# Attention values with the values held in the array: every second head by 64x64 quadrants

## The chip, the cores and the metric

The kernel runs on one core of a Trainium2 chip. The core has a matrix engine (TensorE, PE in the profile; its weight loads are listed as PEld), VectorE (DVE), ScalarE (ACT), GpSimd (POOL) and SyncE (SP), which here only issues DMA transfers. Each engine takes its own instructions in program order, and they wait for each other by semaphores. The metric is the device time of one execution in microseconds (us).

## The reference

A layernorm of `x` (2048 x 640) feeds two branches: attention with 32 heads of 192 over a cache of 2048 keys and values, and a gated MLP of width 1536. The result is `x + attention * silu(mlp)`.

```python
xn = layernorm(x)
q = (xn @ wq).reshape(B, Sq, H, Dh)              # H = 32, Dh = 192
scores = einsum("bhqd,bhkd->bhqk", q, k_cache) * Dh ** -0.5
o = einsum("bhqk,bhkd->bhqd", softmax(scores), v_cache)
s = o.reshape(B, Sq, H * Dh) @ wo
g = silu(silu_gated_mlp(xn, w1, w3, w2))
out = x + s * g
```

## The kernel before

Nearly all of the time goes to a loop over heads `h`, in each over four **blocks** `qb` of 512 queries, and in each block over eight **steps** `p`. A step handles 256 keys: key tiles `p` and `p + 8` of 128, kept as the index `t` of 0 and 1. `ROWS` are the two halves of the 128 partitions, 0 to 63 and 64 to 127. All matmuls of the loop use 64 rows of the array and 128 columns; two of them, one on each half of the rows, run side by side.

In a step, `scores` (L472) makes the transposed scores, keys on partitions and queries along the row: the 192 dimensions are three parts of 64, so three pairs of matmuls with 512 columns fill a PSUM tile `st2` of 128x1024. `weights` (L488) is one Exp on ScalarE, with a bound of the scores (`nb`) in place of the row maximum, into a bf16 tile `pT2`; the pool `pp` has four. `values` (L519) loads 64x128 pieces of `pT2` into the array as weights and streams the values `vt`: 192 columns and one column of ones (set in L142), so the 193rd column of each output row is the sum of its probabilities. That is sixteen matmuls of 193 columns a step, in eight pairs, into two PSUM tiles `ob0` and `ob1` (`acc["o"]`), where the two halves of the rows keep apart sums (index `r`). The values of a step are two **parts**, put in the list `parts`; `advance` (L545) first issues the scores and the Exp of a step and then takes parts off the list until three (four where `extra` is given) are left, so the values run one to two steps behind the scores.

At the end of a block `evict` (L493) has VectorE copy one half sum (L500), add the other (L501), take the reciprocal of the ones column (L506), and multiply (L507) into a bf16 stage `ostage`, which holds two heads (`HG`) of one block; after the second head SP stores it to `o_scr`.

In the second step of each block `extra` runs `project_chunk` (L340) for the same block of the next head: twenty matmuls of 512 columns (L361) into a tile `ps`, two casts on VectorE (L363, L364), and copies on GpSimd (L367, L371) that put halves of the queries on the other partitions. `ps` and `st2` come from one pool, `ps_st`, of two buffers. A step later VectorE takes the maxima of the queries (L375), and in the later steps those of the next head's keys (`next_keys`, L386), both for the bound. `load_head` (L150) loads keys (a DMA transpose on SP), values and weights of the head after the next at the start of a head. In odd heads `swiglu_chunk` (L454) works on a piece of the MLP that rides along in the projection. Instructions wrapped in `pin` keep their program order.

After the loop come the rest of the MLP (L704, L911, L927) and the output product with `wo` (L847, L891), which reads `o_scr` by DMA transposes.

Of the kernel before, what the change touches and what calls it, by code (L numbers as in the profile page):

```python
# [30 lines left out]
def _kernel_impl(ctx, tc, A_x, A_k_cache, A_v_cache, A_wq, A_wo, B_w1, B_w3, B_w2, out):  # L31
# [124 lines left out]
    with ExitStack() as actx:  # L156
        qp = actx.enter_context(tc.tile_pool(name="qp", bufs=2))
        pp = actx.enter_context(tc.tile_pool(name="pp", bufs=4))
# [150 lines left out]
        def start_head(h):  # L309
            L = loads.pop(h)  # L310
            heads[h] = dict(
                h=h, L=L,
# [27 lines left out]
        def project_chunk(h, qb, cast=nc.vector.tensor_copy, mid=()):  # L340
# [6 lines left out]
            if h == 0 and qb > 0:  # L347
                by_halves(halves, lambda t, c: wq[:, t, c, :], qs, nc.scalar.copy if qb == 1 else nc.vector.tensor_copy, steps((parts.pop(0),), *mid))
# [8 lines left out]
            else:  # L357
                for s in range(2 * DC):
                    for t in range(2):
                        xs = xnT if s % 2 == t else xnS  # L360
                        pin(nc.tensor.matmul(halves[t], lhsT=wq[ROWS[t], s, :], rhs=xs[ROWS[t], s // 2, qs],  # L361
                                             start=(s == 0), stop=(s == 2 * DC - 1)))
            pin(cast(out=qA[:, qs], in_=halves[0]))  # L363
            pin(cast(out=qF[:, qs], in_=halves[1]))  # L364
# [107 lines left out]
        def scores(hd, qb, p, fill=(0, 0, 0), st2=None):  # L472
# [8 lines left out]
            for s, step in enumerate(steps):  # L481
                keep_busy(fill[s])
                for t, (k, q) in enumerate(step):
                    pin(nc.tensor.matmul(st2[:, t * 512:(t + 1) * 512], lhsT=k, rhs=q[ROWS[t], qs],  # L484
                                         start=(s == 0), stop=(s == 2)))
            return st2

        def weights(st2, nb):  # L488
            pT2 = pp.tile([P, 1024], BF16, tag="pT2", name="pT2")
            pin(nc.scalar.activation(out=pT2[:], in_=st2[:], func=ACT.Exp, scale=SCALE, bias=nb[:]))  # L490
            return pT2

        def evict(hd, qb, b, ob):  # L493
            h, hg = hd["h"], hd["h"] % HG
            if b == 0 and hg == 0:
                acc[qb] = stp.tile([P, 4, HG * DH], BF16, tag=f"ostage{qb}", name="ostage")
            ostage = acc[qb]
# [5 lines left out]
            def rest():  # L503
# [3 lines left out]
                pin(nc.vector.tensor_tensor(out=ostage[:, b * 2:b * 2 + 2, hg * DH:(hg + 1) * DH], in0=osum[:, :, 0:DH],  # L507
                                            in1=rl.unsqueeze(2).to_broadcast([P, 2, DH]), op=ALU.mult))
                if b == 1 and hg == HG - 1:
                    g0 = h - hg  # L510
# [117 lines left out]
        def next_part():  # L628
            parts.pop(0)()
# [517 lines left out]
```

## Time and profile before

| what | time |
|---|---|
| device time, median of 3 runs (lowest to highest) | 1936.98 us (1936.93 to 1937.15) |
| span of the profiled execution, first to last instruction | 1935.5 us |
| end of the last scores matmul (end of the loop over heads) | about 1644 us |
| one block in the middle of the loop | 12.67 us |
| Exp of one step (128x1024) on ScalarE, mean | 1.113 us |

A row of a group of instructions reads: line, engine, operation, names written and read, shapes, count; then busy time in us and the mean duration in ns; then the idle time of the engine just before them and what ended it. A row of the chain of waits or of the timeline begins with the start in us from the span's start and the duration in us; `x6` is the number of instructions merged into it. `64*128` on a matmul is the part of the array in use, rows by columns. Matmuls are pipelined: one of 512 columns is listed with 0.38 us, though the next pair begins 0.216 us later.

### The profile page before, as it was taken

Reading aid. Unit: us, or ns where it says so; the run is one execution under the profiler, and the core shown is the slowest. Engines: PE = TensorE matmul, PEld = TensorE weight load, DVE = VectorE, ACT = ScalarE, POOL = GpSimd, SP = SyncE. Lnnn points to the kernel's source line nnn. Section 1 sums busy time; section 2 is a strip of 40 time slices with the busy share of each in tenths; the row PEclk is TensorE's granted clock in tenths of the full one; section 3 lists DMA queues with packets and bytes.
Section 4 is the critical chain, followed back from the end, with each engine's and each line's share of the span. In section 5 each row is a group of like instructions: output and inputs, shape, how many; then the busy total and the mean of one; then the engine's idle time right before and its main releaser. Section 6 shows DMA issues by size and latency. Waiting matters only on the chain.

```text
span 1935.5 us, 59521 instructions
## 1 busy us (share of the span) xinstructions
PE 1927.5 (100%) x26720; PEld 1266.1 (65%) x26743; DVE 1091.5 (56%) x2240; ACT 1213.5 (63%) x1173; POOL 457.9 (24%) x757
## 2 busy tenths in 40 slices
PE   9999999999999999999999999999999999999999
PEld 5666666666666666666666677666666666454446
DVE  8665656565656565666655666656665655521111
ACT  7777777777767677777777777777777777210000
POOL 3432222222222222233222222222222220000000
PEclk9999999999999999999999999999999999999999
DMA  7621313121212222242223222213131102946763
GB/s 172 133 71 41 80 41 79 42 71 38 59 41 65 52 55 62 57 95 68 63 50 71 50 71 49 71 41 79 42 79 38 43 10 90 262 93 144 166 151 77
DMA packets 340355, 148.31 MB, mean 77 GB/s; under 512 B 291632, under 2 KB 333584, under 8 KB 340096
## 3 DMA queue, kind: packets, MB, share of 16 engines
q1 hardware_dynamic: 327152, 114.84, 25.7%
q0 software_dynamic: 8256, 24.58, 4.8%
q10 hardware_dynamic: 4688, 5.05, 0.8%
q8 instruction: 210, 3.44, 0.8%
q14 instruction: 49, 0.40, 0.1%
HBM read 54.26 MB, written 31.98 MB: 45 GB/s over the span
## 4 chain that ended last, share of the span: by engine, by line
PE 99%; ACT 0%; issue 0%; DVE 0%; POOL 0%
PE obank L530 35%; PE st L484 34%; PE ps L361 14%; PE ps_s L891 8%; PE ps_s L847 3%; PE ps_f L911 2%; PE ps_gu L704 1%; PE ps_f L927 1%; PE ps L729 0%; PE ps L330 0%; PE fill L207 0%; PE pst L272 0%; PE ps_gu L330 0%; ACT xnT L273 0%; POOL qS L367 0%
## 5 line engine op out<-in xcount | busy, mean ns | idle before, releaser
L490 ACT ACTIVATE pT<-st,nb 128x1024 bf16<-128x1024 f32 x1016 | 1130.8, 1113 | 435.1 <-PE st L484 434.7
L530 PEld LDWEIGHTS <-pT 64*128 64x128 bf16 x16384 | 713.8, 94 | 242.0 <-ACT pT L490 1.5
L530 PE MATMUL obank<-vt,pT 64*128 64x193 bf16 x16384 | 852.3, 243 | 0.2 <-ACT pT L490 0.2
L500 DVE COPY osum<-obank 128x386 f32<-128x386 f32 x256 | 142.4, 556 | 551.4 <-PE obank L530 551.4
L484 PE MATMUL st<-qS,KM 64*128 64x512 bf16 x1023 | 385.2, 377 | 0.5 <-POOL qS L367 0.5
L484 PE MATMUL st<-qD,KT 64*128 64x512 bf16 x1023 | 385.2, 377 | 0.0
L484 PE MATMUL st<-qS,KT 64*128 64x512 bf16 x1023 | 385.1, 376 | 0.1
L484 PE MATMUL st<-qA,KT 64*128 64x512 bf16 x1023 | 385.2, 377 | 0.0
L484 PE MATMUL st<-qA,KM 64*128 64x512 bf16 x1023 | 385.2, 376 | 0.0
L484 PE MATMUL st<-qF,KT 64*128 64x512 bf16 x1023 | 385.1, 376 | 0.0
L367 POOL COPY qS<-qA 64x512 bf16<-64x512 bf16 x256 | 189.4, 740 | 513.8 <-DVE qA L363 482.3
L484 PEld LDWEIGHTS <-KT 64*128 64x128 bf16 x4096 | 202.2, 94 | 135.8 <-issue 0.6
L361 PE MATMUL ps<-xnT,wq 64*128 64x512 bf16 x1240 | 288.1, 376 | 0.0
L361 PE MATMUL ps<-xnS,wq 64*128 64x512 bf16 x1240 | 287.0, 377 | 0.0
L361 PEld LDWEIGHTS <-wq 64*128 64x128 bf16 x2480 | 120.6, 94 | 116.2
L507 DVE TENSOR_TENSOR ostage<-osum,rl_all 128x384 bf16<-128x384 f32 x256 | 153.4, 599 | 8.8
L891 PE MATMUL ps_s<-oT,wo_sb 128*128 128x512 bf16 x705 | 154.9, 379 | 0.8
L501 DVE TENSOR_TENSOR osum<-osum,obank 128x386 f32<-128x386 f32 x256 | 142.6, 557 | 8.9
L891 PEld LDWEIGHTS <-wo_sb 128*128 128x128 bf16 x720 | 70.4, 98 | 85.0 <-issue 0.2
L386 DVE TENSOR_REDUCE st<-KT 128x1 f32<-128x512 bf16 (+1 forms) x189 | 122.0, 685 | 1.2
L484 PEld LDWEIGHTS <-KM 64*128 64x128 bf16 x2048 | 101.0, 94 | 16.5 <-issue 0.5
L105 POOL DMA_DIRECT2D wq<-in_A_wq_dram x62 | 45.7, 737 | 272.8 <-PE ps L361 260.4
(136 smaller groups left out, 1174.6 us busy)
## 6 DMA issues: line engine op xcount, KB each, us to landing
o_scr<-ostage SPq DMA_DIRECT2D x64, 384.0 KB, 2.8
vt<-in_A_v_cache_dram SPq DMA_DIRECT2D x62, 384.0 KB, 4.9
wo_sb<-in_A_wo_dram POOLq DMA_DIRECT2D x1, 7680.0 KB, 32.6
wq<-in_A_wq_dram POOLq DMA_DIRECT2D x31, 160.0 KB, 3.3
hT_scr<-hblk SPq DMA_DIRECT2D x16, 256.0 KB, 3.0
xnS<-xnT POOLq DMA_DIRECT2D x8, 320.0 KB, 7.0
wq<-in_B_w_dram POOLq DMA_DIRECT2D x31, 80.0 KB, 2.6
wq<-in_A_wq_dram POOLq DMA_DIRECT2D x31, 80.0 KB, 2.9
```

The costliest lines, as they stand in the source:

```text
L105: keep(nc.gpsimd.dma_start(out=wq[ROWS[t], :, c0:c1], in_=w.rearrange("(s p) d -> p s d", p=DT)))
L361: pin(nc.tensor.matmul(halves[t], lhsT=wq[ROWS[t], s, :], rhs=xs[ROWS[t], s // 2, qs], start=(s == 0), stop=(s == 2 * DC - 1)))
L367: keep(nc.gpsimd.tensor_copy(out=qS[ROWS[t], qs], in_=qA[ROWS[1 - t], qs]))
L386: pin(nc.vector.tensor_reduce(out=heads[h]["st"][:, j, k:k + 1], in_=heads[h]["L"]["KT"][:, j, c0:c1], axis=AX.X, op=ALU.max, apply_absolu ...
L484: pin(nc.tensor.matmul(st2[:, t * 512:(t + 1) * 512], lhsT=k, rhs=q[ROWS[t], qs], start=(s == 0), stop=(s == 2)))
L490: pin(nc.scalar.activation(out=pT2[:], in_=st2[:], func=ACT.Exp, scale=SCALE, bias=nb[:]))
L500: pin(nc.vector.tensor_copy(out=osum[:], in_=ov[:, 0, :, 0:DH + 1]))
L501: pin(nc.vector.tensor_tensor(out=osum[:], in0=osum[:], in1=ov[:, 1, :, 0:DH + 1], op=ALU.add))
L507: pin(nc.vector.tensor_tensor(out=ostage[:, b * 2:b * 2 + 2, hg * DH:(hg + 1) * DH], in0=osum[:, :, 0:DH], in1=rl.unsqueeze(2).to_broadcas ...
L530: pin(nc.tensor.matmul(acc["o"][b][:, r, (j % 2) * 256:(j % 2) * 256 + DH + 1], lhsT=pT2[ROWS[r], t * 512 + j * P:t * 512 + (j + 1) * P], ...
L847: pin(nc.tensor.matmul(ps, lhsT=oT[:, k, :], rhs=wo_sb[:, k, c0:c1], start=(k == 0), stop=(k == OC - 1)))
L891: pin(nc.tensor.matmul(ps_of[d], lhsT=wo_sb[:, k, d * P:(d + 1) * P], rhs=part(k // KQ)[:, k % KQ, :], start=(k == 0), stop=(k == OC - 1)))
```

## The change

In the even heads from 2 to 30 (`in_quads`, fifteen of 32) the roles in the values product are exchanged: 64x64 pieces of the values `vt` are loaded into the array, and the probabilities `pT2` stream past with 512 columns. Four such matmuls make a group, one for each quadrant (rows `r`, columns `c`); a step has three groups, `high(0)`, `high(1)` for the first 128 value dimensions and `low` for the last 64 of both key tiles. The output is now transposed, value dimensions on partitions. Scores, projections and the last MLP piece in these heads are issued as 64x64 quadrants as well, so twice as many matmuls; at the border between two heads the first two steps and the projection keep the shape of the head before (`before["quads"]`).

The ones column is not used there. VectorE adds up `pT2` instead (`row_sums`): pairs of steps, then joins, then the two key tiles, in bf16; SP turns the 128x512 result with a DMA transpose, and VectorE reduces it and takes the reciprocal (`scale`). At the end of a block ScalarE copies one half sum of the high part (`evict_high`), VectorE copies one and adds two (`evict_low`), and SP turns the 128x1024 bf16 result with a DMA transpose into `ox`. GpSimd adds the two key tiles' low parts and multiplies by the reciprocals into `ostage`. The steps of this work that belong to no fixed place are held in a list, `chores`, from which `do_chores` takes up to `QUOTA[p]` after step `p`; `clock` counts steps, and `scale` is due six steps after `ends`.

`pT2` now holds two steps, with three buffers in place of four. The second cast of a projection goes to ScalarE while a quadrant head runs. `step` takes the place of `advance` from head 1 on: it empties the list of the block before ahead of a projection, and keeps five parts waiting in quadrant heads (three elsewhere). `stage` and `staged` make and store `ostage` when both heads of a pair have delivered. The pools of the new tiles (`aq`) are closed in the last head, and the pool `hTp` of the MLP opens there instead of after head 0.

The core of the diff:

```diff
+    def in_quads(h):
+        return 1 < h < H - 1 and h % 2 == 0
...
-        pp = actx.enter_context(tc.tile_pool(name="pp", bufs=4))
+        pp = actx.enter_context(tc.tile_pool(name="pp", bufs=3))
...
+        def by_steps(halves, w, qs, quads):
+            for s in range(2 * DC):
+                for c in ROWS if quads else (slice(0, P),):
+                    for t in range(2):
+                        xs = xnT if s % 2 == t else xnS
+                        pin(nc.tensor.matmul(halves[t][c, :], lhsT=w[ROWS[t], s, c], rhs=xs[ROWS[t], s // 2, qs],
+                                             start=(s == 0), stop=(s == 2 * DC - 1)))
...
-                for s in range(2 * DC):
-                    for t in range(2):
-                        xs = xnT if s % 2 == t else xnS
-                        pin(nc.tensor.matmul(halves[t], lhsT=wq[ROWS[t], s, :], rhs=xs[ROWS[t], s // 2, qs],
-                                             start=(s == 0), stop=(s == 2 * DC - 1)))
+                by_steps(halves, wq, qs, quads)
             pin(cast(out=qA[:, qs], in_=halves[0]))
-            pin(cast(out=qF[:, qs], in_=halves[1]))
+            pin((cast_low or cast)(out=qF[:, qs], in_=halves[1]))
...
-                for t, (k, q) in enumerate(step):
-                    pin(nc.tensor.matmul(st2[:, t * 512:(t + 1) * 512], lhsT=k, rhs=q[ROWS[t], qs],
-                                         start=(s == 0), stop=(s == 2)))
+                for c in ROWS if quads else (slice(0, P),):
+                    for t, (k, q) in enumerate(step):
+                        pin(nc.tensor.matmul(st2[c, t * 512:(t + 1) * 512], lhsT=k[:, c], rhs=q[ROWS[t], qs],
+                                             start=(s == 0), stop=(s == 2)))
             return st2
 
-        def weights(st2, nb):
-            pT2 = pp.tile([P, 1024], BF16, tag="pT2", name="pT2")
-            pin(nc.scalar.activation(out=pT2[:], in_=st2[:], func=ACT.Exp, scale=SCALE, bias=nb[:]))
+        def weights(st2, nb, p):
+            if p % 2 == 0:
+                acc["w"] = pp.tile([P, 2, 1024], BF16, tag="pT2", name="pT2")
+            pT2 = acc["w"][:, p % 2, :]
+            pin(nc.scalar.activation(out=pT2, in_=st2[:], func=ACT.Exp, scale=SCALE, bias=nb[:]))
...
+        def values_quads(hd, qb, p, pT2):
+            vt = hd["L"]["vt"]
+
+            def sums(b, ts, ch):
+                bank = acc["o"][b]
+                for c, (t, c0) in enumerate(zip(ts, ch)):
+                    for r in range(2):
+                        pin(nc.tensor.matmul(bank[ROWS[c], r, :], lhsT=vt[ROWS[r], t, p, c0:c0 + DT],
+                                             rhs=pT2[ROWS[r], t * 512:(t + 1) * 512],
+                                             start=(p == 0 and (b == 1 or ts[c] == 0)),
+                                             stop=(p == NPAIR - 1 and (b == 1 or ts[c] == 1))))
+
+            def high(t):
+                if p == 0 and t == 0:
+                    acc["o"] = [ps_o.tile([P, 2, 512], F32, tag=f"ob{b}", name=f"obank{b}") for b in range(2)]
+                sums(0, (t, t), (0, DT))
+                if p == NPAIR - 1 and t == 1:
+                    evict_high(hd, qb, acc["o"][0])
+
+            def low():
+                sums(1, (0, 1), (P, P))
+                if p == NPAIR - 1:
+                    evict_low(hd, qb, acc["o"])
+
+            fs = [lambda: high(0), low, lambda: high(1)]
+            if p in (0, NPAIR - 1):
+                fs = [fs[0], fs[2], fs[1]]
+            return [((hd["h"], qb), f) for f in fs]
...
+        def evict_high(hd, qb, bank):
+            acc["oa"] = aq["one"].tile([P, 512], F32, tag="oa", name="oa")
+            pin(nc.scalar.copy(out=acc["oa"][:], in_=bank[:, 0, :]))
+
+        def evict_low(hd, qb, banks):
+            oa = acc["oa"]
+            ol = aq["one"].tile([P, 512], F32, tag="ol", name="ol")
+            ot = aq["two"].tile([P, 2, 512], BF16, tag="ot", name="ot")
+            ox = aq["two"].tile([P, 2, 4, P], BF16, tag="ox", name="ox")
+            pin(nc.vector.tensor_copy(out=ol[:], in_=banks[1][:, 0, :]))
+            pin(nc.vector.tensor_tensor(out=ot[:, 0, :], in0=oa[:], in1=banks[0][:, 1, :], op=ALU.add))
+            pin(nc.vector.tensor_tensor(out=ot[:, 1, :], in0=ol[:], in1=banks[1][:, 1, :], op=ALU.add))
+            nc.sync.dma_start_transpose(out=ox[:].rearrange("p a j c -> p (a j) c"), in_=ot[:].rearrange("p a q -> p (a q)"))
+            hd["ox"][qb] = ox
+
+        def later(wait, f, *a):
+            chores.append((clock[0] + wait, f, a))
+
+        def add(out, a, b):
+            pin(nc.vector.tensor_tensor(out=out, in0=a, in1=b, op=ALU.add))
+
+        def row_sums(hd, qb, p, w):
+            sm = hd["sums"]
+
+            def pairs():
+                t = aq["tree"].tile([P, 1024], BF16, tag="tree", name="tree")
+                add(t[:], w[:, 0, :], w[:, 1, :])
+                sm.append(t)
+
+            def join():
+                b = sm.pop()
+                add(sm[-1][:], sm[-1][:], b[:])
+
+            def ends():
+                t = sm.pop()
+                e = aq["two"].tile([P, 512], BF16, tag="e", name="e")
+                add(e[:], t[:, 0:512], t[:, 512:1024])
+                eT = aq["two"].tile([P, 4, P], BF16, tag="eT", name="eT")
+                nc.sync.dma_start_transpose(out=eT[:], in_=e[:])
+                later(6, scale, eT)
+
+            def scale(eT):
+                h, hg = hd["h"], hd["h"] % HG
+                ox = hd["ox"].pop(qb)
+                rs = stt.tile([P, 4], F32, tag="rs", name="rs")
+                pin(nc.vector.tensor_reduce(out=rs[:], in_=eT[:], axis=AX.X, op=ALU.add))
+                rl = rl_all[:, h * NQT + qb * 4:h * NQT + qb * 4 + 4]
+                pin(nc.vector.reciprocal(out=rl, in_=rs[:]))
+                ostage = stage(h, qb)
+                low = aq["two"].tile([P, 4, DT], F32, tag="low", name="low")
+                nc.gpsimd.tensor_tensor(out=low[:], in0=ox[:, 1, :, 0:DT], in1=ox[:, 1, :, DT:P], op=ALU.add)
+                for src, c0, c1 in ((ox[:, 0, :, :], 0, P), (low[:], P, DH)):
+                    nc.gpsimd.tensor_tensor(out=ostage[:, :, hg * DH + c0:hg * DH + c1], in0=src,
+                                            in1=rl.unsqueeze(2).to_broadcast([P, 4, c1 - c0]), op=ALU.mult)
+                staged(h, qb)
+
+            later(1, pairs)
+            if p % 4 == 3:
+                later(1, join)
+            if p == NPAIR - 1:
+                later(1, join)
+                later(1, ends)
+
+        clock = [0]
+        chores = []
+        aq = {}
+        QUOTA = (2, 0, 1, 2, 1, 1, 1, 1)
+
+        def do_chores(n):
+            for _ in range(n):
+                ready = [c for c in chores if c[0] <= clock[0]]
+                if ready:
+                    chores.remove(ready[0])
+                    ready[0][1](*ready[0][2])
 
         heads = {}
         parts = []
         late = []
 
         def advance(hd, qb, p, extra=None):
-            pT2 = weights(scores(hd, qb, p), hd["nb"][qb])
+            pT2 = weights(scores(hd, qb, p), hd["nb"][qb], p)
             parts.extend(values(hd, qb, p, pT2))
             while len(parts) > (4 if extra else 3):
-                parts.pop(0)()
+                next_part()
             if extra:
                 extra()
             while late:
                 late.pop(0)()
+
+        def step(hd, qb, p, extra=None):
+            me = (hd["h"], qb)
+            first = qb == 0 and p < 2
+            st2 = scores(hd, qb, p, quads=before["quads"] if first else hd["quads"])
+            old = [k for k, _ in parts if k != me]
+            old_quads = bool(old) and heads_quads(old[0][0])
+            if p == 1 and old_quads:
+                while parts[0][0] != me:
+                    next_part()
+            pT2 = weights(st2, hd["nb"][qb], p)
+            parts.extend((values_quads if hd["quads"] else values)(hd, qb, p, pT2))
+            if hd["quads"] and p % 2 == 1:
+                row_sums(hd, qb, p, acc["w"])
+            if p == 0:
+                while sum(k != me for k, _ in parts) > (2 if old_quads else 1):
+                    next_part()
+            elif p == 1:
+                while parts[0][0] != me:
+                    next_part()
+            else:
+                while len(parts) > (5 if hd["quads"] else 3):
+                    next_part()
+            if extra:
+                extra()
+            while late:
+                late.pop(0)()
+            clock[0] += 1
+            do_chores(QUOTA[p])
+
...
+        astack = ExitStack()
+        for name, n in (("one", 1), ("two", 2), ("tree", 4)):
+            aq[name] = astack.enter_context(tc.tile_pool(name=f"aq_{name}", bufs=n, side="right"))
...
+            hd.update(sums=[], ox={})
...
+                    quads = before["quads"] if qb == 0 else hd["quads"]
                     if h + 1 < H:
-                        post.append(project_chunk(h + 1, qb))
+                        post.append(project_chunk(h + 1, qb, quads=quads, cast_low=nc.scalar.copy if hd["quads"] else None))
...
-                    advance(hd, qb, p, extra if p == 1 else None)
+                    step(hd, qb, p, extra if p == 1 else None)
...
+            before["quads"] = hd["quads"]
```

More of the change, by code (lines that the diff above doesn't have):

```diff
@@ L608, in lead @@
             vals[0].pop(0)()
-            vals.append(values(hd, 0, 3, weights(scores(hd, 0, 3), nb)))
+            vals.append([f for _, f in values(hd, 0, 3, weights(scores(hd, 0, 3), nb, 3))])
             vals[1].pop(0)()
@@ L612, in lead @@
             st2 = scores(hd, 0, 4)
-            vals.append(values(hd, 0, 4, weights(st2, nb)))
+            vals.append([f for _, f in values(hd, 0, 4, weights(st2, nb, 4))])
             for v in vals[:4]:
@@ L622, in lead @@
             vals[4].pop(0)()
-            parts.extend(vals[4])
+            parts.extend(((0, 0), f) for f in vals[4])
             for i in (9, 10):
@@ L763, in _kernel_impl @@
                 post = []
+                if (h, qb) == (H - 1, 2):
+                    while chores:
+                        clock[0] += 1
+                        do_chores(1)
+                    astack.close()
+                    acc["hTp"] = fstack.enter_context(tc.tile_pool(name="hTp", bufs=2, side="right"))
                 def extra():
```

62 lines of the change are left out of this document (34 added, 28 removed).

## The prediction

> **What bounds the kernel now.** I read the page first: busy shares, granted clock, chain of waits.
>
> ```profile
> span 1935.5 us, 59521 instructions
> PE 1927.5 (100%) x26720; PEld 1266.1 (65%) x26743; DVE 1091.5 (56%) x2240; ACT 1213.5 (63%) x1173; POOL 457.9 (24%) x757
> PEclk9999999999999999999999999999999999999999
> PE obank L530 35%; PE st L484 34%; PE ps L361 14%; PE ps_s L891 8%; PE ps_s L847 3%; PE ps_f L911 2%; PE ps_gu L704 1%; PE ps_f L927 1%; PE ps L729 0%; PE ps L330 0%; PE fill L207 0%; PE pst L272 0%; PE ps_gu L330 0%; ACT xnT L273 0%; POOL qS L367 0%
> ```
>
> PE is busy all the span at full granted clock, and 83% of the chain is the three lines that the change touches: values (L530), scores (L484), projections (L361). No other engine of computation is above 63%. So the end is set by the columns that PE streams, and by whether PE has to wait. Next the chain by windows: its shares over 305.66 to 1319.66 us (first row), then one block (512 queries of one head, eight steps).
>
> ```profile
> by line: PE obank L530 42.1%; PE st L484 40.9%; PE ps L361 17.0%
> ...
> 799.92 0.65 PE st L484 x6
> 800.56 1.00 PE obank L530 x24
> ...
> 802.21 0.67 PE obank L530 x16
> ...
> 810.43 2.16 PE ps L361 x20
> 812.59 0.65 PE st L484 x6
> ```
>
> The block takes 812.59 - 799.92 = 12.67 us; a row further down gives 50.70 for four, 12.675 each, so the 1014 us hold 80 blocks, 640 steps. Scores are 0.409 x 1014 / 640 = 0.648 us a step, three pairs of matmuls at 0.216; values 0.421 x 1014 / 640 = 0.667, eight pairs at 0.0834; a projection 0.170 x 1014 / 80 = 2.155, ten pairs at 0.2155. A pair fills the two 64x128 halves of the array:
>
> ```profile
> 801.40 0.38 PE L484 MATMUL st<-qS,KM 64*128 64x512 bf16 x1
> 801.40 0.38 PE L484 MATMUL st<-qA,KM 64*128 64x512 bf16 x1
> 801.61 0.38 PE L484 MATMUL st<-qA,KT 64*128 64x512 bf16 x1
> 801.62 0.38 PE L484 MATMUL st<-qS,KT 64*128 64x512 bf16 x1
> 801.83 0.38 PE L484 MATMUL st<-qD,KT 64*128 64x512 bf16 x1
> 801.83 0.38 PE L484 MATMUL st<-qF,KT 64*128 64x512 bf16 x1
> ```
>
> Partners start together, three offsets of 0.00, 0.01 and 0.00 us, and 512 columns take 0.2157 from pair to pair (the mean of the two rates).
>
> **The change, part by part.** *Values.* In the 15 even heads from 2 to 30 a step loses eight pairs of 193 columns (192 and the ones) and gets three groups of four quadrants with 512. If four quadrants run together as two halves do, the step costs 3 x 0.2157 = 0.647 instead of 0.667: 0.020 less in 15 x 32 = 480 steps, **9.6 us gained** (9.1 to 10.1 by the rounding of the shares). More is excluded, since 1536 columns still pass each half.
>
> *Scores and projections there* keep their columns and double their instructions. A group is 8 PE instructions in 0.2157 us, 27 ns each; the values before issued 4 in 0.0834, 21 ns each. So issue fits, and I cost it at nothing. A step has 3 + 3 + 10/8 = 7.25 groups; if each took one ns more, 480 x 7.25 = 3480 groups would cost 3.5 us.
>
> *Weights.* A group loads four 64x64 quadrants.
>
> ```profile
> L530 PEld LDWEIGHTS <-pT 64*128 64x128 bf16 x16384 | 713.8, 94 | 242.0 <-ACT pT L490 1.5
> ...
> 802.05 0.18 PEld L530 LDWEIGHTS <-pT 64*128 64x128 bf16 x4
> ```
>
> One load takes 94 ns, and four (two per half) end within 0.18 us, under the running matmuls. A group with two in line per half needs 188 ns, under 216: hidden, 0, my value, as nearest to this row. All four in line would be 376, 160 ns too many for each group; that is the upper end. [...]
>
> *Changes of shape.* PE goes to quadrants at the third step of such a head and back at the third step of the next: 30 changes. The nearest rows go from halves to the whole array, and back:
>
> ```profile
> 1647.83 0.25 PE L530 MATMUL obank<-vt,pT 64*128 64x193 bf16 x2
> 1648.00 0.39 PE L704 MATMUL ps_gu<-xnT,w_sb 128*128 128x512 bf16 x1
> ...
> 14.28 0.20 PE L427 MATMUL bp<-prb,ones_bf 128*128 128x1 bf16 x2
> 14.42 0.39 PE L484 MATMUL st<-qS,KM 64*128 64x512 bf16 x1
> ```
>
> The first starts 0.17 after a pair that streams for 0.083; the second 0.14 after two matmuls of one column. I take 0.10 each, **3.0 us lost** (0 to 0.14: 0 to 4.2).
>
> *VectorE.* A quadrant block drops two evictions of three operations (L500, L501, L507) and one cast. It gets seven bf16 additions of 1024 and one of 512, a reduction, and three operations of 512 from PSUM.
>
> ```profile
> L500 DVE COPY osum<-obank 128x386 f32<-128x386 f32 x256 | 142.4, 556 | 551.4 <-PE obank L530 551.4
> L507 DVE TENSOR_TENSOR ostage<-osum,rl_all 128x384 bf16<-128x384 f32 x256 | 153.4, 599 | 8.8
> L501 DVE TENSOR_TENSOR osum<-osum,obank 128x386 f32<-128x386 f32 x256 | 142.6, 557 | 8.9
> ...
> L363 DVE CAST qA<-ps x120: 690/692/693, 77.6 to 1585.9; 128x512 bf16<-128x512 f32 x120
> ...
> L375 DVE TENSOR_REDUCE st<-qA x127: 670/677/686, 26.2 to 1587.8; 128x1 f32<-128x512 bf16 x127
> ...
> L466 DVE TENSOR_TENSOR hblk<-pa,qF x64: 416/417/1141, 82.2 to 1614.9; 64x512 bf16<-64x512 bf16 x64
> ...
> sum 50.70, PE 50.70 PEld 34.62 DVE 31.70 ACT 37.17 POOL 13.68; mean PE 12.68 PEld 8.66 DVE 7.93 ACT 9.29 POOL 3.42
> ```
>
> The colon rows give minimum/median/maximum in ns. From 386 to 512 elements the PSUM read grows by 136 ns, 1.08 per element, so 139 are fixed; a bf16 addition of 1024 is then 139 + 2 x (417 - 139) = 695 ns (if the second half ran at 1.08: 970). Added: 7 x 0.695 + 0.417 + 0.677 + 3 x 0.69 = 8.03. Removed: 2 x 1.712 + 0.69 = 4.11. The block goes from 7.93 to 11.85 of 12.675 us: hidden, but 94% full. The tightest place is the first block after a quadrant head. There the three PSUM operations wait for the last group, and behind them stand both casts of the projection: 2.07 + 1.38 = 3.45 us. PE wants the projection's bank back after projection, scores and three values parts, 2.16 + 0.65 + 1.00 = 3.81. The pair and two joins of the last step stand ahead: they begin when its Exp ends, 1.11 after its scores, need 2.09, and PE is 3.03 further on by the last group, so they are about 0.2 late. That leaves 0.2 of cover; I put 0.1 us on each of 15 borders, **1.5 us lost** (0 to 0.8 each, if every operation ran 0.1 longer: 0 to 12).
>
> *ScalarE, GpSimd, SP.*
>
> ```profile
> L490 ACT ACTIVATE pT<-st,nb 128x1024 bf16<-128x1024 f32 x1016 | 1130.8, 1113 | 435.1 <-PE st L484 434.7
> ...
> L363 ACT CAST qA<-ps x8: 585/585/586, 11.2 to 68.8; 128x512 bf16<-128x512 f32 x8
> ...
> L367 POOL COPY qS<-qA x256: 604/622/1008, 12.4 to 1587.3; 64x512 bf16<-64x512 bf16 x128
> ...
> POOL wq L105 <- PE ps L361: 260.4, 27, 9.9
> ...
> KT<-in_A_k_cache_dram SPq DMA_TRANSPOSE x34, 5.6
> ...
> rows<-resT SPq DMA_TRANSPOSE x15, 2.5
> ```
>
> Two copies of 0.585 bring ScalarE to 8 x 1.113 + 1.17 = 10.1 of 12.675; the one ahead of the second step's Exp lies under the projection (without that cover 0.585 a block). GpSimd gets three two-operand products, some 2 us from its copy of 0.62; only the stores wait for them. One behind a weight load that waits 9.9 us still has a block's time, as `ox` has two buffers. SP gets a transpose of 1024 and one of 512 columns a block (2.5 us to land for 512, so some 5 for the other), behind keys that take 5.6. The reduction on VectorE that waits for `eT` comes six steps, 9.5 us, later, and 2.5 + 5.6 still fit, so 0; were it late, the query maxima and the next casts stand behind it. The ring of `pT2` holds six steps instead of four: no wait.
>
> **Sum.** -9.6 + 3.0 + 1.5 = -5.1 us on the execution of span 1935.5. The runs shown have a median of 1936.98, 1.5 more than that span, and I leave that as it is: **1932**.
>
> **The rivals.**
> 1. *Quadrants start one after another, slower.* Of the three offsets above the mean is 0.0033 us. If each of the two further starts of a group adds that, and the next group waits for the last, a group is 6.7 ns longer: 23 us, so 1955. From 5.1 / 3480 = 1.5 ns on the change is lost. For it: no row has more than two starts at once. Against it: pairs pay an offset too, and still follow at 0.2157.
> 2. *VectorE becomes the bound.*
>
> ```profile
> 788.66 1.03 POOL L139 COPY KM<-KT 64x1024 bf16<-64x1024 bf16 x1
> ...
> 788.68 1.43 DVE L507 TENSOR_TENSOR ostage<-osum,rl_all 128x384 bf16<-128x384 f32 x1
> ```
>
> An operation on two SBUF tensors that began just behind a copy on GpSimd took 1.43 us instead of 0.56, while the copy kept its 1.03 (row L466 has such a maximum too). In a quadrant block bf16 additions take 5.3 us of VectorE and GpSimd works some 3.4 + 2 = 5.4, so by chance they meet for 5.3 x 5.4 / 12.675 = 2.3 us. If VectorE loses half of that, its block is 13.0, 0.3 over, and 60 blocks cost 18 us; if all, 14.15 and 88 us. Midway: 1985. Against it: the medians are undisturbed, and PE has buffers ahead. [...]
> 3. *PE waits eat the gain, no change.* At 5.1 / 60 = 0.085 us a block it is gone: 1937. For it: a cover of 0.2 us at the borders. Against it: within a quadrant head one cast moves to ScalarE, so the cover there is 0.7 more.
> 4. *Weights in line, or the column halves take turns* (the change does not do what it says): 160 ns a group are 557 us, 2489; 0.2157 a group are 751 us, 2683. For it: no row shows a quadrant. Against it: the row halves do both side by side.
>
> **Chances.** Forecast 0.43, rivals 0.12, 0.24, 0.13, 0.08. I count a difference over 0.2%, 3.9 us, as told from no change. Faster is the forecast, 0.43; within 0.2% the third rival, 0.13; slower the others, 0.44. The forecast's own range is 1927 (no cost of switches and borders) to 1935. For 8 in 10 I go up over rivals 3 and 1 and take in nearly half of the second: 1927 to 1978.
>
> **What would show it.** Right: values in quadrant heads as three groups of 0.216 in the chain, gaps of about 0.1 at shape changes, VectorE near 11.9 in a quadrant block, chain still 99% PE. Rival 1 shows as groups over 0.217 in scores too, 2 as PE waiting for DVE with additions over 0.7, 4 as groups of 0.37 or 0.43. I am wrong if a quadrant head is not some 0.4 us shorter than its neighbours.

## The result, and the profile after

The changed kernel takes 2108.76 us (median of 4 runs, 2107.14 to 2112.59) against 1937.07 before (1936.93 to 1937.62): a ratio of 1.0889 (95% interval 1.0874 to 1.0905), 172 us slower, where 1932 within 1927 to 1978 was predicted. Lines of the changed kernel: L492 scores, L500 Exp, L550 values by halves, L570 values by quadrants, L348 projection, L370 and L371 its casts, L611 additions of the row sums, L642 to L644 the products on GpSimd, L444 and L447 the last local step of the bound (`ns`) and the all-reduce on GpSimd that makes `nb` of it.

The page of the changed kernel: engines, PE and its clock by slices, the chain, three groups.

```profile
span 2105.8 us, 64373 instructions
...
PE 1960.8 (93%) x28880; PEld 1239.4 (59%) x28903; DVE 1341.7 (64%) x2480; ACT 1264.7 (60%) x1293; POOL 652.4 (31%) x937
...
PE   9998989898999989898989898999989898999999
...
PE 84%; DMA 4%; DVE 4%; issue 4%; ACT 3%; POOL 1%; SPq 0%; POOLq 0%
...
L570 PEld LDWEIGHTS <-vt 64*64 64x64 bf16 x5760 | 201.4, 107 | 116.5 <-DVE ot L603 0.3
...
L642 POOL TENSOR_TENSOR low<-ox 128x256 f32<-128x256 bf16 x60 | 56.9, 948 | 387.0 <-DMA ox<-ot 387.0
...
L611 DVE TENSOR_TENSOR tree<-tree 128x1024 bf16<-128x1024 bf16 x180 | 140.4, 780 | 4.3
```

No engine is full: PE is at 93% instead of 100%, VectorE at 64%. PE's slices drop from 9 to 8 at intervals. So this is neither a slower matmul everywhere nor an engine that became the bound, but a stop at certain places. The waits, with sum, count and longest, name them:

```profile
ACT pT L500 <- POOL nb L447: 152.4, 29, 9.7
POOL nb L447 <- issue: 139.0, 22, 7.1
...
PE ps L348 <- ACT pT L500: 134.4, 29, 9.0
...
ACT qF L371 <- DVE qA L370: 105.3, 60, 2.2
...
POOL ostage L644 <- issue: 93.9, 14, 7.2
```

PE waits 134.4 us ahead of a projection for an Exp, the Exp waits 152.4 for `nb`, 29 times each: once per border between two heads. `nb` itself and the product `ostage` waited for "issue", for nothing that the profile shows, up to 7 us at a time. The chain at the border into a quadrant head (first window) and out of it (second window):

```profile
801.30 0.41 POOL nb L447
...
801.73 1.12 ACT pT L500
...
802.90 2.42 PE ps L348 x20
805.31 0.77 PE st L492 x12
...
808.24 0.65 PE st L492 x12
808.89 0.65 PE obank L570 x12
```

```profile
850.95 6.07 DMA KT<-in_A_k_cache_dram
...
857.09 2.54 issue
859.63 0.41 POOL nb L447
...
861.23 4.29 PE ps L348 x40
865.52 0.75 PE st L492 x6
```

The matmuls did what was forecast: a step of scores and a step of three quadrant groups take 0.65 us each. The loss is at the borders. The transfer of keys on the chain of the second window is no cause: the copies that read these keys (L136, L139) stand behind `nb` in GpSimd's order (the first starts at 861.71), and the transfer only ended in the pause. What ends the pause is `nb`, and the timelines of VectorE and GpSimd show why it is late (in brackets: the idle time just before, and what ended it):

```profile
795.31 0.15 DVE L444 TENSOR_REDUCE ns<-pr 128x1 f32<-128x2 f32 x1
...
801.30 0.40 POOL L447 PARTITION_ALL_REDUCE nb<-ns  x1 [5.95 <-issue]
...
846.80 0.15 DVE L444 TENSOR_REDUCE ns<-pr 128x1 f32<-128x2 f32 x1
...
852.50 1.06 POOL L644 TENSOR_TENSOR ostage<-low,rl_all 128x256 bf16<-128x256 f32 x1
...
859.63 0.40 POOL L447 PARTITION_ALL_REDUCE nb<-ns  x1 [6.06 <-issue]
```

Into the quadrant head `nb` starts 5.84 us after `ns` has ended (795.46 to 801.30), out of it 12.68 us (846.95 to 859.63). The first is an idle GpSimd; the second is 6.6 us of work ahead of it in GpSimd's queue (weight transfer, copies, products that had waited for the transposed outputs) and then 6.06 us idle. In the raw records two instructions of GpSimd's sequencer stand in this idle time:

```
852.50  POOL   L644  TENSOR_TENSOR ostage<-low,rl_all
853.76  POOLq  L447  MODIFY_POOL_CONFIG
853.80  POOLq  L447  MODIFY_POOL_CONFIG
859.63  POOL   L447  PARTITION_ALL_REDUCE nb<-ns
```

The same pair stands ahead of a product on two tensors that follows an all-reduce: 59 pairs in the loop, one for each change between the two kinds. In the kernel before, no GpSimd instruction of the loop is an operation on two tensors, and the pair stands nowhere in its loop. There the timelines of VectorE, GpSimd and ScalarE, and a row of the waits, read:

```profile
829.11 0.15 DVE L437 TENSOR_REDUCE ns<-pr 128x1 f32<-128x2 f32 x1
...
829.46 0.65 POOL L440 PARTITION_ALL_REDUCE nb<-ns  x1 [0.33 <-DVE ns L437]
...
834.25 1.11 ACT L490 ACTIVATE pT<-st,nb 128x1024 bf16<-128x1024 f32 x1 [0.22 <-PE st L484]
```

```profile
POOL warm L579 <- issue: 6.0, 1, 6.0
```

`nb` is there at 830.11, 4.1 us ahead of the first Exp that needs it. And the clue was in the waits before: the kernel's first all-reduce (`warm`, L579, ahead of the loop; nothing reads its result) waited 6.0 us for "issue". In the raw records the same pair of MODIFY_POOL_CONFIG stands 5.8 us ahead of it.

The clock adds to it. Windows of the changed kernel over a projection behind a short pause, one inside a quadrant head and the one behind the long pause (busy time and count by engine, then the granted clock):

```profile
802.90:805.31 2.41, 2.41 (x24) 1.69 (x27) 0.90 (x2) 0.95 (x1) 1.12 (x2) 1.00 1.02 157
828.70:830.86 2.16, 2.16 (x44) 1.44 (x40) 2.04 (x4) 1.43 (x2) 1.72 (x2) 1.00 0.00 0
861.23:865.52 4.29, 4.29 (x42) 2.09 (x43) 1.28 (x2) 1.94 (x3) 2.67 (x5) 0.54 0.52 98
```

The same projection takes 4.29 us at a clock of 0.54 instead of 2.16 at 1.00. Behind the short pause the clock stays at 1.00; the 2.41 there are no loss of clock. The granted clock fell to 0.5 at each of the 15 pauses of 7.45 us or more and at none of 1.46 or less, and no pause of the changed kernel's loop lies between.

From PE's start times, pauses over 0.3 us ahead of the loop's projections and scores: 15 out of quadrant heads with 120.0 us (7.45 to 9.12, most near 7.9), 14 into them with 17.2 (1.05 to 1.46), and 15 of 0.34 to 0.72 at the end of a quadrant head's first block with 5.6. From its first matmul to the next scores a projection takes 3.71 to 4.41 us behind the long pauses instead of 2.16, 28.2 more in all, and 2.35 behind the short ones, 2.7 more. That is 120.0 + 17.2 + 5.6 + 28.2 + 2.7 = 173.7 us; less what the steps gain (some 2 us, below), the 172 are accounted for.

### The profile page after: what moved, and what is told of

The parts are those of the page before. It is cut to its first block, busy times and chain, and to the rows that moved or that the text cites. A ratio compares the mean times of both kernels' runs of the same rounds, so it can differ in the third digit from the quotient of the medians.

```text
span 2105.8 us, 64373 instructions
## 1 busy us (share of the span) xinstructions
PE 1960.8 (93%) x28880; PEld 1239.4 (59%) x28903; DVE 1341.7 (64%) x2480; ACT 1264.7 (60%) x1293; POOL 652.4 (31%) x937
## 4 chain that ended last, share of the span: by engine, by line
PE 84%; DMA 4%; DVE 4%; issue 4%; ACT 3%; POOL 1%; SPq 0%; POOLq 0%
PE st L492 29%; PE obank L550 17%; PE ps L348 13%; PE obank L570 12%; PE ps_s L1056 7%; DMA KT<-in_A_k_cache_dram 4%; ACT pT L500 3%; PE ps_s L1012 2%; PE ps_f L1076 2%; DVE tree L611 1%; PE ps_gu L864 1%; PE ps_f L1092 1%; POOL nb L447 1%; DVE ol L601 1%; DVE st L393 1%
## 5 line engine op out<-in xcount | busy, mean ns | idle before, releaser
L500 ACT ACTIVATE pT<-st,nb 128x1024 bf16<-128x1024 f32 x1016 | 1126.2, 1114 | 431.9 <-PE st L492 240.9
L550 PEld LDWEIGHTS <-pT 64*128 64x128 bf16 x8704 | 378.8, 94 | 130.1 <-ACT pT L500 1.5
L550 PE MATMUL obank<-vt,pT 64*128 64x193 bf16 x8704 | 452.9, 243 | 0.2 <-ACT pT L500 0.2
L348 PE MATMUL ps<-xnT,wq 64*64 64x512 bf16 (+1 forms) x1830 | 315.0, 407 | 126.6 <-ACT pT L500 126.6
L570 PE MATMUL obank<-pT,vt 64*64 64x512 bf16 x5760 | 402.1, 376 | 0.0
L492 PE MATMUL st<-qS,KM 64*64 64x512 bf16 (+1 forms) x1503 | 398.4, 378 | 3.5 <-ACT qF L371 3.2
L492 PE MATMUL st<-qA,KT 64*64 64x512 bf16 (+1 forms) x1503 | 397.7, 376 | 0.0
L492 PE MATMUL st<-qD,KT 64*64 64x512 bf16 (+1 forms) x1503 | 397.7, 376 | 0.0
L492 PE MATMUL st<-qA,KM 64*64 64x512 bf16 (+1 forms) x1503 | 390.1, 378 | 0.0
L492 PE MATMUL st<-qS,KT 64*64 64x512 bf16 (+1 forms) x1503 | 388.3, 376 | 0.1
L492 PE MATMUL st<-qF,KT 64*64 64x512 bf16 (+1 forms) x1503 | 388.1, 376 | 0.0
L492 PEld LDWEIGHTS <-KT 64*64 64x64 bf16 (+1 forms) x6016 | 237.9, 102 | 141.1 <-issue 1.3
L348 PE MATMUL ps<-xnS,wq 64*64 64x512 bf16 (+1 forms) x1830 | 310.5, 408 | 0.0
L348 PEld LDWEIGHTS <-wq 64*64 64x64 bf16 (+1 forms) x3660 | 163.8, 111 | 243.6 <-issue 155.1
L570 PEld LDWEIGHTS <-vt 64*64 64x64 bf16 x5760 | 201.4, 107 | 116.5 <-DVE ot L603 0.3
L611 DVE TENSOR_TENSOR tree<-pT 128x1024 bf16<-128x1024 bf16 x240 | 195.0, 823 | 87.9 <-ACT pT L500 87.1
L642 POOL TENSOR_TENSOR low<-ox 128x256 f32<-128x256 bf16 x60 | 56.9, 948 | 387.0 <-DMA ox<-ot 387.0
L492 PEld LDWEIGHTS <-KM 64*64 64x64 bf16 (+1 forms) x3008 | 124.1, 102 | 68.1 <-issue 27.9
L611 DVE TENSOR_TENSOR tree<-tree 128x1024 bf16<-128x1024 bf16 x180 | 140.4, 780 | 4.3
```

The costliest lines, as they stand in the source:

```text
L348: pin(nc.tensor.matmul(halves[t][c, :], lhsT=w[ROWS[t], s, c], rhs=xs[ROWS[t], s // 2, qs], start=(s == 0), stop=(s == 2 * DC - 1)))
L492: pin(nc.tensor.matmul(st2[c, t * 512:(t + 1) * 512], lhsT=k[:, c], rhs=q[ROWS[t], qs], start=(s == 0), stop=(s == 2)))
L500: pin(nc.scalar.activation(out=pT2, in_=st2[:], func=ACT.Exp, scale=SCALE, bias=nb[:]))
L550: pin(nc.tensor.matmul(acc["o"][b][:, r, (j % 2) * 256:(j % 2) * 256 + DH + 1], lhsT=pT2[ROWS[r], t * 512 + j * P:t * 512 + (j + 1) * P], ...
L570: pin(nc.tensor.matmul(bank[ROWS[c], r, :], lhsT=vt[ROWS[r], t, p, c0:c0 + DT], rhs=pT2[ROWS[r], t * 512:(t + 1) * 512], start=(p == 0 and ...
L611: pin(nc.vector.tensor_tensor(out=out, in0=a, in1=b, op=ALU.add))
```

## The experiments

Theory L ("load", the author's name for such an idle time): GpSimd stands idle for some 6 us whenever it goes from an all-reduce to an operation on two tensors, or back, as the 5.95 and 6.06 us ahead of `nb` suggest. Rivals were Q, the queue: `nb` stands behind copies, products and their transposes; V: VectorE has too much to do; and that quadrants cost more than they save. All comparisons are with the kernel before, at 1937.0 to 1937.1 in the same runs.

**No all-reduce in the loop** (from head 2 on `nb` is the local product of each partition, not the sum over the partitions; the rest as in the changed kernel):

```diff
+            if 2 in heads or 3 in heads or 0 not in heads:
+                nc.gpsimd.tensor_copy(out=nb[:], in_=ns[:])
+            else:
+                keep(nc.gpsimd.partition_all_reduce(nb[:], ns[:], P, bass_isa.ReduceOp.add))
```

> From head 2 on the sum over partitions in the bound (GpSimd's PARTITION_ALL_REDUCE, 0.40 us) is left out: GpSimd copies each partition's own part into nb instead. All else of the changed kernel stays, the order on GpSimd and its waits too. [...] Theory Q (nb is late because the additions waiting for a DMA and the products stand ahead of it in GpSimd's queue, and the gap is only queueing): that queue stays, so 2090 to 2110. Theory V (VectorE is the bound): unchanged, 2100 to 2110.

Measured 1963.59 us, 1.0133 (1.0116 to 1.0150). By theory L 144 us were to go, 15 x (6.1 + 2.1) at the borders out of a quadrant head (the idle time, and the projection's 4.29 us instead of 2.16) and 15 x 1.4 at those into one (the short pauses), to near 1965 (1950 to 1975). So it came: 145 of the 172 us go with one instruction; Q and V as main causes fall. The products, the queue and VectorE's work are all still there. What is left at the border out of a quadrant head is the queue; its chain:

```profile
786.91 3.06 DMA ox<-ot
...
794.24 2.43 POOL ostage L647 x2
796.67 0.60 POOL nb L448
...
798.46 2.35 PE ps L348 x40
```

The products still wait for the transposed outputs, and `nb` for the products, but no row has 6 us of issue, PE pauses 1.29 us, and the projection takes 2.35. At the 15 borders of this kind PE pauses 1.29 to 2.17 us, 23 us in all, most of the 26.6 that this version still loses.

**The products on VectorE, in place** (the all-reduce stays):

```diff
-                nc.gpsimd.tensor_tensor(out=low[:], in0=ox[:, 1, :, 0:DT], in1=ox[:, 1, :, DT:P], op=ALU.add)
+                pin(nc.vector.tensor_tensor(out=low[:], in0=ox[:, 1, :, 0:DT], in1=ox[:, 1, :, DT:P], op=ALU.add))
...
-                    nc.gpsimd.tensor_tensor(out=ostage[:, :, hg * DH + c0:hg * DH + c1], in0=src,
-                                            in1=rl.unsqueeze(2).to_broadcast([P, 4, c1 - c0]), op=ALU.mult)
+                    pin(nc.vector.tensor_tensor(out=ostage[:, :, hg * DH + c0:hg * DH + c1], in0=src,
+                                                in1=rl.unsqueeze(2).to_broadcast([P, 4, c1 - c0]), op=ALU.mult))
```

> The addition and two products per block move from GpSimd to VectorE, at the same places. [...] V: a quadrant block of VectorE grows from 11.85 to about 13.4 of 12.675 us, 0.7 over in 60 blocks, 40 us: 1970 to 1985. If VectorE's work is only late where something waits for it, 1932 to 1950.

Measured 1960.48 us, 1.0119 (1.0102 to 1.0136), between the two ranges: less than V has it, and more than work that is late at single places was expected to cost. So the all-reduce may stay if the products go: it is the pair of kinds on one engine that costs, not either of them. The long pauses are gone; what is left are pauses up to 0.75 us in quadrant heads, where VectorE is late.

**The same, with the products in the odd head that follows** (one `low`, one `ot`, four `ox`; due by the step counter from the head's first step, `t0`):

```diff
+                chores.append((hd["t0"] + 42 + 5 * qb, products, (ox, rl)))
+
+            def products(ox, rl):
...
+                low = aq["one"].tile([P, 4, DT], F32, tag="low", name="low")
```

> As the one before, but the addition and products of all four blocks of a quadrant head are done on VectorE in the odd head that follows, whose blocks have 8.1 of 12.675 us of it (four buffers of ox, one of ot and of low to make room). L and Q: no border waits, quadrant blocks with 11 us of VectorE: 1930 to 1938. V (the additions themselves are stretched or too late): 1945 to 1970.

Measured 1954.39 us, 1.0088 (1.0072 to 1.0105), in V's range and not in that of L and Q: the remainder is VectorE after all. But it is late at single places. The chain at the end of a quadrant head's first block:

```profile
753.00 0.59 DVE st L393
753.60 0.61 DVE tree L611
...
756.12 0.60 DVE ot L603
756.72 0.61 DVE qA L370
...
757.35 0.59 ACT qF L371
...
757.99 0.84 PE st L492 x12
```

Each row of the chain starts where the one before it ends: a maximum of the next head's keys (L393; four of the six stand in this block), additions, the operations on PSUM, the cast on VectorE and then the cast on ScalarE. PE waits 0.34 us for the last. In the odd head's third block a product stands ahead of an eviction in the same way, for 0.45 and 0.21 us. All pauses of PE over 0.15 us in this loop are of these three kinds, 15.8 us in all.

**Quadrants alone**: row sums, evictions and their transposes left out, zeros stored for these heads. Of the new work on GpSimd only memsets are left.

```diff
-                if p == NPAIR - 1 and t == 1:
-                    evict_high(hd, qb, acc["o"][0])
...
-                    evict_low(hd, qb, acc["o"])
+                    nc.gpsimd.memset(stage(h, qb)[:, :, hg * DH:(hg + 1) * DH], 0.0)
...
-            if hd["quads"] and p % 2 == 1:
-                row_sums(hd, qb, p, acc["w"])
```

> The quadrant heads keep all their matmuls and Exps, but row sums, copies out of PSUM, turns and products are left out (GpSimd sets their outputs to constants). If quadrants run at the rate of the halves, as the sum had it: -9.6 us for the values and +3 to +4 for 30 changes of shape, 1930 to 1932. If the matmuls themselves had become slower, above 1940.

Measured 1937.47 us (1935.92 to 1938.71), 1.000 (0.999 to 1.001): no gain, 5.5 to 7.5 us above what was expected. Some 3 us of that are the edit's own. Its memsets of `rl_all` are not pinned, and GpSimd ran all 60 of them at the start of the kernel, between the copies that the first bound needs (13 at 10.32 us, then the row below); the first Exp starts at 17.61 us, where it was 14.72 before.

```profile
11.95 1.52 POOL L585 MEMSET rl_all<- 128x4 f32 x47
```

In the loop two heads take 101.28 us instead of 101.40, so 15 x 0.12 = 1.8 us are gained there. The chain, and ScalarE's timeline behind the same projection, show where the rest of the loop's gain stays:

```profile
765.51 0.65 PE st L492 x12
766.16 0.86 PE obank L570 x16
767.02 0.74 PE st L492 x12
...
766.28 0.58 ACT L371 CAST qF<-ps 128x512 bf16<-128x512 f32 x1 [2.20 <-DVE qA L370]
```

The second scores behind a projection take 0.74, though none of the change's work on VectorE is there to be late: they need the projection's PSUM buffer, and that comes free only when both casts have ended. ScalarE's cast begins when VectorE's has ended, and lasts to 766.86; the scores' first matmul starts at 766.92. 0.09 in three of four blocks is 45 x 0.09 = 4.0 us. The shape changes cost 0.12 into a quadrant head (0.77 instead of 0.65 in the chain above) and 0.10 out of it (0.75), 15 x 0.22 = 3.3 us: 9.6 - 4.0 - 3.3 = 2.3, where 1.8 were measured and the 9.6 itself is good to 0.5.

**The load in the kernel before.** To see theory L without any of the change, one instruction was put into the kernel before, ahead of the all-reduce: an addition of two 128x2 tiles on GpSimd, and in a second kernel a copy of the same tile. Nothing reads `z`.

```diff
+            if 0 not in heads:
+                z = stt.tile([P, 2], F32, tag="z", name="z")
+                nc.gpsimd.tensor_tensor(out=z[:], in0=pr[:], in1=pr[:], op=ALU.add)
             keep(nc.gpsimd.partition_all_reduce(nb[:], ns[:], P, bass_isa.ReduceOp.add))
```

> The kernel before with one more GpSimd instruction a head (heads 3 to 31, 29 of them): an addition of two 128x2 tiles, its result unused, between the row of VectorE that ends the bound's local product and the all-reduce that makes the bound nb. Nothing else is changed. [...]

> As the run with two swaps, but the added instruction is a copy of the same 128x2 tile. All theories: 1935 to 1941, since a copy was seen on both sides of an all-reduce without a load. If it costs as much as the addition, the place or the added wait is the cause, not the kind of operation, and theory L falls.

The addition: 2276.58 us, 1.1749 (1.1731 to 1.1767). The copy: 1937.09 us, 1.000 (0.999 to 1.001). GpSimd's timeline with the addition, then with the copy:

```profile
862.98 0.49 POOL L442 TENSOR_TENSOR z<-pr 128x2 f32<-128x2 f32 x1 [7.19 <-DVE rl_all L509]
...
870.42 0.40 POOL L443 PARTITION_ALL_REDUCE nb<-ns  x1 [6.95 <-issue]
```

```profile
829.65 0.69 POOL L442 COPY z<-pr 128x2 f32<-128x2 f32 x1
830.32 0.38 POOL L443 PARTITION_ALL_REDUCE nb<-ns  x1
```

An addition of 0.49 us brings two idle times of 7.19 and 6.95 us, the copy none. (That the first is put down to `rl_all` L509 is an inference that misleads: VectorE had ended that at 853.3, and `pr`, which the addition reads, at 855.7.) So the price hangs on the change between these two kinds of instruction, at 128x2 elements as at the 128x256 of the products, and without the changed kernel's queue. What GpSimd does in that time was not shown. For the addition theory L had 2213 us (2150 to 2240): 29 borders with 7.4 us of pause and 2.1 more for the projection behind it, as at the clock of 0.54 above; the other side, a longer queue or a slower all-reduce as the cause, had 1935 to 1941. The size was 64 us over the 2213, since a change here takes some 7 us and not 6, twice, so that PE pauses 8.0 to 10.5 us at a border, mostly about 9.5, instead of 7.4.

**A version without loads and with VectorE spread out.** From the version with products in the odd head: two maxima of keys in each of three blocks, products in the middle of a block, and four parts instead of five kept back in the steps behind a projection:

```diff
-                chores.append((hd["t0"] + 42 + 5 * qb, products, (ox, rl)))
+                chores.append((hd["t0"] + 36 + 8 * qb, products, (ox, rl)))
...
-                while len(parts) > (5 if hd["quads"] else 3):
+                while len(parts) > ((4 if p < 4 else 5) if hd["quads"] else 3):
...
-                        elif p > 3 and key_slots and (h > 1 or qb > 0):
+                        elif (p > 3 if h == 1 else p in (5, 6)) and key_slots and (h > 1 or qb > 0):
```

> The version with the products on VectorE in the following odd head, with three changes of order alone: maxima of the keys two a block over three blocks instead of four and two; the products due after the fifth step of each block of the odd head instead of every fifth step; four parts kept back in the third and fourth step of a quadrant block instead of five, so that one group more lies between projection and the scores that need its buffer. Theory L/Q (what is left of the loss is VectorE late at single places, and the two casts in a row that come 0.09 too late in 45 blocks): no load, no idle at borders beyond the changes of shape: -9.6 for the values, +3.6 for 30 changes of shape, 0 to 5 for what remains: 1931 to 1937. Rival V (VectorE has too much to do in a quadrant head as a whole: 11.85 us and 1.36 for two maxima against 12.6): the lateness only moves, 1943 to 1955.

Measured 1932.15 us, 0.9975 (0.9965 to 0.9985), as expected of L and Q: the lateness did not move elsewhere (two pauses over 0.15 us are left in the loop, both of 0.2), so VectorE's work fits a quadrant head. Of the 22.2 us to the version before it the pauses make 15.8 and the 45 waits of 0.09 some 4. And with both casts on ScalarE in quadrant heads:

```diff
-                        post.append(project_chunk(h + 1, qb, quads=quads, cast_low=nc.scalar.copy if hd["quads"] else None))
+                        post.append(project_chunk(h + 1, qb, quads=quads, cast=nc.scalar.copy if hd["quads"] else nc.vector.tensor_copy))
```

> The version with spread maxima and products, and both casts of a projection in quadrant heads on ScalarE. VectorE falls by 0.69 to some 12.5 of 12.6 in the blocks with two maxima. Theory L/Q: 1930 to 1936. Rival S (ScalarE, 10.7 of 12.6 us a block, now makes PE wait: the Exp of the third step comes 0.6 later): +0.1 to 0.3 in 60 blocks against the version before it, 1938 to 1953.

Measured 1930.35 us (1930.03 to 1930.62), 0.9965 (0.9951 to 0.9979): faster than the changed kernel and, by 0.35%, than the one before, 6.7 us below it. Its page, windows of a quadrant head and of the odd head that follows, and the chain behind a projection:

```profile
PE 1921.8 (100%) x28880; PEld 1157.2 (60%) x28903; DVE 1376.5 (71%) x2600; ACT 1298.4 (67%) x1353; POOL 457.1 (24%) x757
```

```profile
734.20:784.40 50.20, 50.20 (x932) 27.72 (x928) 40.76 (x70) 41.62 (x45) 13.64 (x23) 1.00 0.36 68
784.40:835.20 50.80, 50.80 (x792) 34.54 (x784) 40.56 (x84) 37.33 (x36) 15.04 (x24) 1.00 0.36 81
```

```profile
747.22 0.65 PE st L492 x12
747.86 1.08 PE obank L570 x20
748.94 0.65 PE st L492 x12
```

With five groups (1.08) instead of four (0.86) between the two scores the second takes 0.65 again, as it did in the version before this one. The two heads take 101.00 us instead of 101.40, 15 x 0.40 = 6.0 us. By the values and the shape changes alone a pair of heads should gain 9.6 / 15 - 0.22 = 0.42. The rival that ScalarE would now make PE wait fell: the time lies below its range, no pause of PE over 0.15 us is left in the loop, and ScalarE is busy 41.6 of 50.2 us.

## Why the prediction was wrong

- **The step that failed is GpSimd's**: "GpSimd gets three two-operand products, some 2 us from its copy of 0.62; only the stores wait for them", costed at nothing. It cost 168 of the 172 us: the pauses at the borders and the slower projections behind them (120.0 + 17.2 + 28.2 + 2.7). Its second half is false: `nb` of the next head stands behind these products in GpSimd's order, the first Exp waits for `nb`, and PE for the Exp. And the price was wrong, because a new kind of instruction was priced by its neighbours' duration: the three products take 2.8 us a block instead of 2 (0.60 to 1.39 each), and they bring two idle times of 5.9 to 7.5 us to each border, one ahead of `nb` and one ahead of the next product, of which PE pays the first. The runs show both halves: without the all-reduce 145 us are gone, and the queue is worth 1.29 to 2.17 us of PE's time at a border out of a quadrant head. The products' own wait for the transposed output (387.0 us in all, some of it beside such an idle time) was not named either. None of the prediction's four rivals contains an idle time between two kinds of operation (5.95 and 6.06 us ahead of `nb` in the two windows).
- **The range** failed with it. All bounds of it came from PE and VectorE; the unknown operation on GpSimd had no upper end, though the wait of 6.0 us at `warm` was in the profile of before.
- **Values, scores, projections: held.** Three groups in 0.65 us, as forecast, and a gain of 0.40 a pair of heads in the last version, where 0.42 is left of the 9.6 us after the shape changes; rivals 1 (a group over 0.217) and 4 (weights in line, or the column halves in turn) are refuted by the chain. Weight loads of 64 columns took 107 ns (94 for 128) and stay hidden: the groups keep their 0.216 us.
- **Changes of shape: held**, 0.12 into and 0.10 out of a quadrant head where 0.10 was taken, within 0 to 0.14: 3.3 instead of 3.0 us.
- **Borders and VectorE: mis-sized, with one false reason.** The 1.5 us at "the first block after a quadrant head" were looked for at the wrong place: the first block *of* a quadrant head, where four key maxima stand, costs 0.35, 5.6 us in all. In the version with the products on VectorE in the odd head, such places cost most of the 22 us between 1954.39 and 1932.15. The block as a whole fits: 40.76 / 4 = 10.2 us in the last version, with both casts gone, where 11.85 - 0.69 = 11.16 was worked out. The sum added up listed durations of 0.68 to 0.70 us, but these overlap: in the chain of the version with the products in the odd head such an operation takes 0.60 or 0.61. Rival 2 is thus half right: VectorE never is the bound, but late by its order. Its mechanism, additions stretched by GpSimd, is small: a mean of 780 ns a join with the products on GpSimd, 697 with them on VectorE, and a median of 692 in both.
- **ScalarE: the reason was false.** "one cast moves to ScalarE, so the cover there is 0.7 more" took the two casts as side by side. They run one after the other, since in the program ScalarE's cast waits for VectorE's (row `ACT qF L371 <- DVE qA L370`, 60 times), and in a quadrant head less work stands between the two scores behind a projection (0.86 us instead of 1.00). That is the 0.09 in three of four blocks, 4 us.
- **What it would show.** Groups of 0.216 and gaps of about 0.1 at shape changes came. "VectorE near 11.9" did not (10.2 in the last version), nor did "chain still 99% PE" (84%). Its own test, "a quadrant head some 0.4 us shorter than its neighbours", fails in the changed kernel, where the two heads take 112.7 us on average instead of 101.40, and holds in the last version (50.20 against 50.80, a shape change in each).
- **What is luck.** The forecast's own range, 1927 to 1935, holds the last two versions only. They have another order and the products on VectorE, which the prediction did not plan. That 1932.15 is so near to 1932 is in part chance: the 1.5 us for the borders did not occur, and about as much is lost elsewhere in the loop of that version (two heads take 101.09 there, 0.09 more than in the last one).

## What to carry to other kernels

When an edit puts a kind of operation on an engine that has not run it in the loop, ask what that engine does between two kinds, and who waits for the next instruction in its order; the duration of a neighbouring operation is no upper bound. A wait "for issue" of several us in the profile, even a single one (here 6.0 us at `warm`), is a price tag: look for what would repeat it. And when a large loss is found, the small ones behind it (a maximum ahead of a cast, one group too few behind a projection) decide whether the change gains anything: here the 24 us from 1954 to 1930.

## What the runs showed of the hardware that was not expected

- GpSimd was idle each time it went between a partition all-reduce and an operation on two tensors, in either direction, even for 128x2 elements: for 5.9 to 7.5 us at 44 of the 59 changes of the changed kernel (ahead of the other 15 a transfer was late, 9.8 to 14.5), and for 7.1 us on average, up to 8.0, at the 58 changes with the addition in the kernel before. Copies ran on either side without it (the copy kernel: 1.000). The idle time is listed as "issue", or put down to a releaser that ended long before.
- Four 64x64 quadrants streamed 512 columns in 0.216 us as two halves do, with weights of 64 columns loaded in 107 ns beneath. A change between halves and quadrants cost 0.10 to 0.12 us.
- After the 15 pauses of 7.45 to 9.12 us the granted clock fell to one half for 6.8 or 10.2 us each, and the projection behind them took 3.71 to 4.41 us instead of 2.16. After the 14 pauses of 1.05 to 1.46 us it stayed at 1.00, and the projection took 2.35.
